# Decay attention in 64-token chunks from the fifth step on, ahead of two mixture layers on one core

## The chip, the cores and the metric

The kernel runs on one NeuronCore of one Trainium2 chip. The time is the device time of one execution in microseconds (us); lower is better. Before the change the median of 3 runs is 934.72 us (934.62 to 934.89).

## The reference: what is computed

There are 4 batches, 8 heads, 768 tokens, head size 48. Attention is a recurrence with a decaying state; its output, reordered to 3072 tokens of 384 numbers, goes through two feed-forward layers of width 2048.

```python
for t in range(S):                       # S = 768
    cur = einsum('bhd,bhe->bhde', u * kt, vt)
    y[:, :, t] = einsum('bhd,bhde->bhe', rt, state + cur)
    state = w * state + einsum('bhd,bhe->bhde', kt, vt)
x = y.transpose(0, 2, 1, 3).reshape(3072, 384)
h = x @ w_in;   x = relu(h)**2 @ w_out           # layer 1
h = x @ w_in2;  out = (h - tanh(h)) @ w_out2     # layer 2
```

The program doesn't walk token by token. It cuts the tokens into chunks. Within a chunk, token t sees token s < t through a masked score matrix (r times powers of w, against k times inverse powers), itself through r·(u*k) on the diagonal, and all earlier chunks through the state.

## The kernel before, in words

**Blocks and steps.** The 3072 tokens form 6 blocks j of 512 tokens; a block holds the same 128-token chunk of all 4 batches. Attention is done in 24 steps i, each one chunk of 128 tokens of one batch; step i belongs to block i // 4. A step has two halves d = 2i and 2i+1, each with two pairs of heads. In a pair one head lies on partitions 0 to 47 and the other on 64 to 111.

**Layers.** For each block and each of 16 slices f of the hidden width, `gemm1` (L496) makes h with 9 matmuls of 512 columns, ScalarE and another engine turn h into a high part `ghi` and a low part `glo`, and `gemm2_1` (L536) adds 9 matmuls into three accumulators. One such f of one block is a unit. The program goes through all units of layer 1 and then all of layer 2 (L646), and `gemm1` is issued one or two units ahead of its `gemm2`. In block 0 of layer 1 the weights are also unpacked on the way (`conv0` and `conv2` on ScalarE, L84 and L101; `conv1` on VectorE, L92 and L93; `conv3`, L107, on VectorE or GpSimd). `act1_low` (L525) makes `glo` on VectorE in the first and last block; in blocks 1 to 4 GpSimd makes it (L516).

**Attention in the units.** The first four steps run ahead of everything (`att_c0`, `att_e0`). Block j's units contain the steps of block j+1: in the units f = 0, 1, 3, 4, 6, 7, 9, 10 one half step d each. A half step issues:

- `att_a` (L253, L254): k and r times the tables of powers `tk` and `tr`, on VectorE. From d = 18 on, `att_split` (L272 to L279) also splits both into high and low fp32r parts, on ScalarE and VectorE.
- `att_b`: the scores. To d = 17 four fp32 matmuls of 128 columns (L300), the two heads of a pair on different rows of the array and into different PSUM banks; from d = 18 on six fp32r matmuls of 256 columns (L290).
- `att_s`, `att_d` (L308, L324): the diagonal, a reduction on VectorE and a product with the identity on GpSimd, written to `am`. `att_m` (L342, L335) copies the scores over `am` where the mask `low` is set, on VectorE.
- `att_c`: the output y. Two matmuls with the state `sbd`, a 112x112 matrix with the two heads' states on its diagonal (L422), four with `am` and v (L429), and, except in the last block, four that make the chunk's own k·v (L438).
- `att_e`: y goes to x in high and low parts (L455, L457), and the state is decayed and added to by four VectorE instructions of 48x48 (L463). `pack` moves the last pair of heads to its rows by DMA (L477).

`att_u`, `att_r`, `att_k` (L229, L232, L237) multiply the natural-order r and k by u, k and the decay table; they are put in a list by `nat_push` and taken off one per unit by `nat_pop`.

**What sets the order.** The order is written out by hand (`manual_schedule`); every engine takes its instructions in that order. PSUM banks are fixed: 0 to 2 the accumulators, 3 and 4 h, 5 to 7 attention.

The half step in a unit of block 0 reads:

```python
if att:
    att_c(d); att_e(d); loads(d); pack(d)
gemm2_1(j, f)
if att and d + 2 < NDALL:
    att_b(d + 2); att_dm(d + 2)
```

Of the kernel before, what the change touches and what calls it, by code (L numbers as in the profile page):

```python
# [25 lines left out]
def decay_attention_moe_moe_kernel(  # L26
# [90 lines left out]

    at_ctx = ExitStack()
# [3 lines left out]
    sbd = [ac.tile([GP, NP, GP], F32, name=f"sbd{o}") for o in range(TPB)]  # L122
    zero = ac.tile([GP, GP], BF16, name="zero")
    ident = ac.tile([128, 128], F32, name="ident")
    low = ac.tile([128, 128], F32, name="low")
    ub = ac.tile([128, DM], F32, name="ub")
    kt_tab = ac.tile([128, H, D], F32, name="kt_tab")
# [45 lines left out]

    def table_b():
# [4 lines left out]
        nc.scalar.activation(out=wdec, in_=vtab[:, :, C - 1:C], func=AF.Copy)  # L179
# [6 lines left out]
    def table_c():  # L186
# [12 lines left out]
        tv = kt_tab.rearrange("p (P two) d -> p two P d", two=2)  # L199
# [3 lines left out]
    def fill(n):  # L203
        t = bank(1, "warm")
        for _ in range(n):
            nc.tensor.matmul(t[0:GP, 0:256], lhsT=zero, rhs=low[0:GP].bitcast(BF16), start=True, stop=True)

    def setup_pool():
# [19 lines left out]
    def att_u(i, eng):  # L228
        eng.tensor_tensor(flat(rn_t[i]), flat(rn_t[i]), ub, op=ALU.mult)  # L229

    def att_r(i, eng):
        eng.tensor_tensor(flat(rn_t[i]), flat(rn_t[i]), flat(kv_t[i][:, 0]), op=ALU.mult)  # L232

    def att_k(i, eng):
        kn = flat(kv_t[i][:, 0])
        if i // TPB != NCH - 1:
            eng.tensor_tensor(kn, kn, flat(kt_tab), op=ALU.mult)  # L237

    nat_q = []

    def nat_push(i, eng):
        if i < NTAU:
            nat_q.extend([(att_u, i, eng), (att_r, i, eng), (att_k, i, nc.gpsimd)])

    def nat_pop(n=1):
        for _ in range(min(n, len(nat_q))):
            fn, i, eng = nat_q.pop(0)
            fn(i, eng)

    def att_a(d, eng=None):  # L250
        i, e = divmod(d, 2)
# [8 lines left out]
    def open_split():  # L260
        t = cv.tile([128, 2 * DM, 2], F32R, tag="raw", name="fr", bufs=3).rearrange("p x two -> p (x two)")
        nc.gpsimd.memset(t[0:GP, 512:1536].bitcast(F32), 0.0)
        ks = t[0:GP, 0:512].rearrange("p (x z s) -> p x z s", x=2, z=2)
        rs = t[0:GP, 512:1536].rearrange("p (x z a t) -> p x z a t", x=2, z=2, a=2)
        fr.append((ks, rs))

    def att_split(d):
        i, e = divmod(d, 2)
        q = slice(2 * e, 2 * e + 2)
        ks, rs = fr[d % 3]  # L270
        r, k = rk_t[i][:, 0, q], rk_t[i][:, 1, q]
        nc.scalar.activation(out=ks[:, 0], in_=k, func=AF.Copy)  # L272
        nc.vector.tensor_tensor(ks[:, 1], k, ks[:, 0].bitcast(F32), op=ALU.subtract)  # L273
        for a in range(2):
            s = slice(64 * a, 64 * a + D)
# [72 lines left out]
    def att_dm(d):  # L348
        if d % 2 == 0:
            att_s(d // 2)  # L350
# [602 lines left out]
```

## Time and profile before

| | us |
|---|---|
| median of 3 runs | 934.72 |
| profiled execution | 935.4 |
| its span, first to last instruction | 933.7 |
| TensorE busy | 907.2 (97%) |
| VectorE busy | 729.7 (78%) |
| ScalarE busy | 642.6 (69%) |
| GpSimd busy | 251.2 (27%) |
| mean granted TensorE clock | 0.989 of full speed |

The span falls into stretches: to about 41 us the first four attention steps run with little else, to 122 us block 0 of layer 1 runs with its weights being unpacked, to 473 us blocks 1 to 4 run with attention steps in them, to 527 us the last block of layer 1, and from there layer 2. Attention after the change is in the stretch from about 37 us to 473 us. PE is TensorE in the rows, DVE VectorE, ACT ScalarE, POOL GpSimd. An fp32 matmul shows as two records, so a group of 4 matmuls is x8; fp32r and bf16 matmuls show as one.

### The profile page before, as it was taken

To read this page: it belongs to the slowest core of one execution; us is meant where nothing else is said; L and a number is where in the kernel's file an instruction comes from. 1 tells how busy PE (TensorE), PEld (TensorE's weight loads), DVE (VectorE), ACT (ScalarE), POOL (GpSimd) and SP (SyncE) were. 2 spreads that over 40 slices of the span, in tenths; PEclk is the share of its full clock that TensorE was granted. 3 is DMA by queue.
4 is the path that set the end of the run, shared out by engine and by line. 5 is a ranking of instruction groups with operands and counts; after the bars stand their busy time and mean duration, and the time that the engine had idled before them with its cause. 6 is when DMAs were issued, how large, how long until landed. Compare 5 with 4: busy or idle time off the path is not lost.

```text
span 933.7 us, 13137 instructions
## 1 busy us (share of the span) xinstructions
PE 907.2 (97%) x4748; PEld 745.8 (80%) x4748; DVE 729.7 (78%) x1201; ACT 642.6 (69%) x1150; POOL 251.2 (27%) x216
## 2 busy tenths in 40 slices
PE   6889999999999999999999999999999999999998
PEld 6666778888888788888888778888888888888886
DVE  6898866882874678173167789999999999999997
ACT  3655665455554555554478797898888988988986
POOL 5832425552654445353202011001001001000000
PEclk7999999999999999999999999999999999999999
DMA  8845422221311212110446210010010100100000
GB/s 239 253 148 191 151 83 85 79 68 37 95 55 50 81 54 95 38 50 10 174 149 222 68 57 11 1 57 12 24 33 12 57 12 1 57 12 1 35 1 34
DMA packets 28801, 67.50 MB, mean 72 GB/s; under 512 B 4929, under 2 KB 11969, under 8 KB 28737
## 3 DMA queue, kind: packets, MB, share of 16 engines
q1 hardware_dynamic: 28592, 66.47, 21.9%
q8 instruction: 37, 0.61, 0.3%
q10 hardware_dynamic: 144, 0.20, 0.1%
q14 instruction: 28, 0.22, 0.1%
HBM read 55.25 MB, written 9.44 MB: 69 GB/s over the span
## 4 chain that ended last, share of the span: by engine, by line
PE 86%; DVE 7%; ACT 3%; DMA 1%; issue 1%; POOL 1%; SPq 0%; DVEq 0%; ACTq 0%; POOLq 0%
PE h L496 39%; PE acc L536 20%; PE o L646 20%; PE sc L290 2%; PE y L429 2%; PE y L422 2%; DMA kvt<-in_nat_dram 1%; DVE am L342 1%; DVE rkt L254 1%; PE sc L300 1%; DVE rkt L253 1%; DVE glo L525 1%; PE y L438 1%; DVE hy L592 1%; DVE raw L93 0%
## 5 line engine op out<-in xcount | busy, mean ns | idle before, releaser
L496 PE MATMUL h<-xt,w 128*128 128x512 f32 x864 | 215.6, 394 | 0.0
L496 PE MATMUL h<-xs,w 128*128 128x512 f32 x864 | 211.4, 389 | 0.0
L496 PEld LDWEIGHTS h<-xs,w 128*128 128x128 f32 x864 | 162.2, 188 | 34.0
L496 PEld LDWEIGHTS h<-xt,w 128*128 128x128 f32 x864 | 161.0, 190 | 33.5
L510 ACT ACTIVATE g<-h 128x512 f32<-128x512 f32 x96 | 57.2, 596 | 146.9 <-PE h L496 146.8
L536 PE MATMUL acc<-ghi,w 128*128 128x512 f32 x576 | 153.3, 398 | 0.3 <-ACT x2s L552 0.3
L646 PE MATMUL o<-ghi,w 128*128 128x512 f32 x576 | 148.8, 390 | 0.3 <-ACT ghi L617 0.3
L646 PEld LDWEIGHTS o<-ghi,w 128*128 128x128 f32 x576 | 107.7, 188 | 24.0 <-ACT ob L657 1.3
L536 PEld LDWEIGHTS acc<-ghi,w 128*128 128x128 f32 x576 | 104.9, 188 | 23.8 <-ACT g L510 1.1
L516 POOL TENSOR_TENSOR glo<-g,ghi 128x512 fp32r<-128x512 f32 x64 | 85.8, 1340 | 136.1 <-ACT ghi L513 61.8
L569 POOL TENSOR_TENSOR xs<-x2f,xs 128x512 fp32r<-128x512 f32 x18 | 24.4, 1354 | 316.6 <-DVE xs L568 316.6
L536 PE MATMUL acc<-glo,w 128*128 128x512 f32 x288 | 84.2, 394 | 6.8 <-DVE glo L525 6.8
L593 ACT ACTIVATE th<-h 128x512 f32<-128x512 f32 x96 | 57.5, 599 | 41.9 <-DVE hy L592 41.9
L646 PE MATMUL o<-glo,w 128*128 128x512 f32 x288 | 84.2, 394 | 2.0 <-DVE glo L623 1.9
L606 DVE SCALAR_TENSOR_TENSOR hy<-q,hy 128x512 f32<-128x512 f32 x96 | 78.2, 814 | 0.1
L592 DVE SCALAR_TENSOR_TENSOR hy<-h,y 128x512 f32<-128x512 f32 x96 | 66.0, 687 | 13.5 <-ACT y L590 13.4
L324 POOL TENSOR_TENSOR am<-ident,bt 128x512 f32<-128x512 f32 x44 | 50.0, 1137 | 90.4 <-DVE bt L308 69.6
L273 DVE TENSOR_TENSOR fr<-rkt,fr 112x256 fp32r<-112x256 f32 x30 | 38.8, 1294 | 42.7 <-ACT fr L272 42.7
L596 DVE TENSOR_TENSOR th<-h,th 128x512 f32<-128x512 f32 x96 | 66.2, 689 | 5.9 <-ACT th L593 0.7
L611 DVE COPY_PREDICATED hy<-mask,th 128x512 f32<-128x512 uint8 x96 | 70.8, 737 | 0.0
L536 PEld LDWEIGHTS acc<-glo,w 128*128 128x128 f32 x288 | 53.8, 188 | 20.7 <-DVE glo L525 9.8
L594 ACT ACTIVATE q<-y,ba 128x512 f32<-128x512 f32 x96 | 68.7, 715 | 0.0
(105 smaller groups left out, 1380.1 us busy)
## 6 DMA issues: line engine op xcount, KB each, us to landing
raw<-in_w_dram SPq DMA_DIRECT2D x32, 768.0 KB, 4.3
rkt<-in_rk_dram SPq DMA_DIRECT2D x23, 448.0 KB, 4.3
kvt<-in_nat_dram SPq DMA_DIRECT2D x23, 384.0 KB, 4.6
x2d<-x2s SPq DMA_DIRECT2D x18, 256.0 KB, 2.3
x2f<-x2d SPq DMA_DIRECT2D x18, 256.0 KB, 3.0
out_dram<-ob SPq DMA_DIRECT2D x18, 256.0 KB, 2.2
rnt<-in_nat_dram SPq DMA_DIRECT2D x23, 192.0 KB, 2.5
xt<-ys SPq DMA_DIRECT2D x120, 16.0 KB, 1.8
```

The costliest lines, as they stand in the source:

```text
L324: nc.gpsimd.tensor_tensor(am_t[d].rearrange("p (a z) t -> p a z t", a=2), ident[:, None, None, :].to_broadcast([128, 2, 2, C]), hd.to_broa ...
L496: nc.tensor.matmul(h, lhsT=w_in(layer, f, part, kk), rhs=x[:, xpart, kk, :], start=(n == 0), stop=(n == 3 * KK - 1),)
L510: nc.scalar.activation(out=g, in_=h, func=AF.Relu)
L516: nc.gpsimd.tensor_tensor(lo, g, hi.bitcast(F32), op=ALU.subtract)
L536: nc.tensor.matmul(acc[j][m], lhsT=w_out(1, f, part, m * 128, (m + 1) * 128), rhs=g, start=(f == 0 and n == 0), stop=(f == NF - 1 and n == 2),
L592: nc.vector.scalar_tensor_tensor(out=hy, in0=h, scalar=PK, in1=y, op0=ALU.mult, op1=ALU.mult)
L593: nc.scalar.activation(out=th, in_=h, func=AF.Tanh)
L594: nc.scalar.activation(out=q1, in_=y, func=AF.Square, bias=p2["ba"], scale=1.0)
L596: nc.vector.tensor_tensor(th, h, th, op=ALU.subtract)
L606: nc.vector.scalar_tensor_tensor(out=hy, in0=q2, scalar=PD, in1=hy, op0=ALU.add, op1=ALU.mult)
L611: nc.vector.copy_predicated(hy, mask, th)
L646: nc.tensor.matmul(acc[j][m], lhsT=w_out(2, f, part, m * 128, (m + 1) * 128), rhs=g, start=(f == 0 and n == 0), stop=(f == NF - 1 and n == 2),
```

## The change

From step 4 on a step is done in one go and not in two halves, and its 128 tokens are cut into two subchunks c of 64. Steps 0 to 3 keep the old code under the names `lead_*`. For the others:

- **Scores** (`att_b`): 16 fp32 matmuls (4 pairs, 2 subchunks, 2 heads) of 48 rows by 64 by 64 columns. The two heads of a pair are on different rows and different column halves of the array, and write the two halves of one PSUM bank (5).
- **k·v of each subchunk** (`att_v`): 16 fp32 matmuls of 64 rows by 64 by 48 columns into bank 6.
- **Output** (`att_c`): 16 fp32 matmuls of 64 by 64 columns. The state and v are stacked in one stationary tile `vs` (state on one head's 48 partitions, v of the 64 tokens on the other 64), and decayed r and the masked scores in one moving tile `ra`, so that one matmul gives both terms. Bank 7.
- **State** (`state_0`, `state_1`): kept as 112 x 4 x 48. VectorE decays and adds it in four instructions of 112x192, and ScalarE copies it into `vs` (four of 48x192).
- `att_a` is one VectorE product for k and two for r; the splitting into fp32r parts is gone. `att_d` writes the diagonal into `ra` (two GpSimd products of 64x512), `att_m` copies scores over it (two of 64x512).
- Visits are at f = 1, 4, 7, 10: `att_b` and `att_v` of step i+1, then `att_c` of step i, all in front of that unit's `gemm2`. `att_a` and `state_0` of step i+2 are issued two units after a visit, at f = 3, 6, 9 and 0. `nat_push` also lists `att_s` and `att_d`, and `nat_pop` takes two per unit.
- v and k come in separate transfers (5 a step in place of 3), and the first four steps' inputs lie in tiles that later hold weights, no longer in the rotating buffers. `table_d` makes a decay table for 64 tokens; VectorE clears the padding of the new tiles at the start.

The core of the diff:

```diff
-    sbd = [ac.tile([GP, NP, GP], F32, name=f"sbd{o}") for o in range(TPB)]
+    L = C // 2
+    GPS = NP * D
...
+    vs_p = [ac.tile([128, 2, VW], F32, name=f"vs{q}") for q in range(NV)]
+    kn_p = [ac.tile([128, VW], F32, name=f"kn{q}") for q in range(2)]
+    ra_p = [ac.tile([128, 2, NP, 2, L], F32, name=f"ra{q}") for q in range(2)]
...
+            nc.sync.dma_start(out=rk_t[i], in_=rk[i])
+            nc.sync.dma_start(out=rn_t[i], in_=nat[i, :, 0])
+            nc.sync.dma_start(out=kn_t[i][:, 0:DM], in_=nat[i, :, 1])
+            for a in range(2):
+                q = slice(64 * (1 - a), 64 * (2 - a))
+                nc.sync.dma_start(out=vs_t[i][q, a, 0:DM], in_=nat[i, q, 2])
...
+        k = sub(rk_t[i][:, 1])
+        win = slice(L // 2, C - L // 2)
+        (eng or nc.vector).tensor_tensor(k, k, tab(tk[:, :, win], GP), op=ALU.mult)
+        for a in range(2):
+            q = slice(64 * a, 64 * a + D)
+            nc.vector.tensor_tensor(ra_t[i][q, a], sub(rk_t[i][q, 0]), tab(tr[q][:, :, win], D), op=ALU.mult)
...
+            nat_q.extend([
+                lambda: att_u(i, G), lambda: att_r(i, G), lambda: att_s(i),
+                lambda: att_k(i, G), lambda: att_d(i, 0), lambda: att_d(i, 1),
+            ])
...
+    def att_b(i):
+        sc_t[i] = sc = pbank(i, 0, "sc").rearrange("p (P c t) -> p P c t", P=NP, c=2)
+        for p in range(NP):
+            for c in range(2):
+                for a in range(2):
+                    q = slice(64 * a, 64 * a + D)
+                    nc.tensor.matmul(
+                        sc[half(a), p, c, :], lhsT=rk_t[i][q, 1, p, c * L:(c + 1) * L], rhs=ra_t[i][q, a, p, c, :],
+                        start=True, stop=True,
+                    )
...
+    def att_v(i):
+        pv_t[i] = pv = pbank(i, 1, "pv")[:, 0:2 * GPS].rearrange("p (c P d) -> p c P d", c=2, P=NP)
+        for c in range(2):
+            for p in range(NP):
+                x = (c * NP + p) * D
+                for a in range(2):
+                    nc.tensor.matmul(
+                        pv[64 * a:64 * a + 64, c, p, :],
+                        lhsT=kn_t[i][half(a), x:x + 64], rhs=vs_t[i][half(a), a, x:x + D],
+                        start=True, stop=True,
+                    )
...
+    def state_1(i):
+        pv = pv_t.pop(i)[0:GP]
+        s = a2.tile([GP, NP, D], F32, tag="s1", name="s1", bufs=1)
+        nc.vector.tensor_tensor(s, dec_t.pop(i), pv[:, 0], op=ALU.add)
+        put_state(i, 1, s)
+        if i // TPB < NCH - 1:
+            m = st_m[i % TPB]
+            decay(m, s)
+            nc.vector.tensor_tensor(m, m, pv[:, 1], op=ALU.add)
...
+    def att_c(i):
+        y_t[i] = y = pbank(i, 2, "y").rearrange("p (P c t) -> p P c t", P=NP, c=2)
+        for p in range(NP):
+            for c in range(2):
+                for a in range(2):
+                    n = GP if a else 128
+                    x = (c * NP + p) * D
+                    nc.tensor.matmul(
+                        y[64 * a:64 * a + 64, p, c, :], lhsT=vs_t[i][0:n, a, x:x + 64], rhs=ra_t[i][0:n, a, p, c, :],
+                        start=True, stop=True,
+                    )
...
+            if layer == 1 and j + 1 < NB and f - 2 in (-2, 1, 4, 7):
+                i = TPB * (j + 1) + visit.get(f - 2, -1) + 2
+                if i < NTAU:
+                    att_a(i)
+                    state_0(i)
             if att:
-                if j == 0:
-                    a_to(min(d + 3, DR - 1))
-                att_c(d)
-                att_e(d)
-                loads(d)
-                pack(d)
+                i = TPB * (j + 1) + visit[f]
+                if i + 1 < NTAU:
+                    att_b(i + 1)
+                    att_v(i + 1)
+                att_c(i)
+                att_e(i)
+                pack(i)
+                load(i + 3)
...
-            if att and d + 2 < NDALL:
-                att_b(d + 2)
-                att_dm(d + 2)
-                if d % 2 == 0:
-                    nat_push(d // 2 + 2, G)
+            if att and i + 1 < NTAU:
+                att_m(i + 1)
+                state_1(i + 1)
+                nat_push(i + 2)
```

How TensorE's order changes: in block 1, before the change, a half step's scores stand between two units and its output behind the next `gemm1`:

```order
L536 MATMUL acc_2272<-glo,w_6_816 128x512
L290 MATMUL sc<-fr 128x256 x6
L496 MATMUL h<-xt,w_9_996 128x512 x9
L422 MATMUL y<-rkt,sbd_89 112x128 x2
L429 MATMUL y<-am,kvt 48x128 x4
L438 MATMUL y<-kvt 48x48 x4
L536 MATMUL acc_2270<-ghi,w_7_895 128x512
```

This comes eight times a block. At the same place after the change there is one piece, four times a block:

```order
L619 MATMUL acc_1558<-glo,w_6_858 128x512
L579 MATMUL h<-xt,w_9_1051 128x512 x9
L351 MATMUL sc<-ra_105,rkt 64x64 x16
L362 MATMUL pv<-vs_101,kn_103 64x48 x16
L413 MATMUL y<-ra_104,vs_100 64x64 x16
L619 MATMUL acc_1556<-ghi,w_7_971 128x512
```

The scores and the k·v of one step now stand directly ahead of the output of the step before it, and there are 48 small matmuls a step where there were 32 (12 of 256 columns and 20 of 48 or 128).

VectorE's order where block 0 begins, before the change (`bt` is the diagonal of the step, `glo` the low part that unit 0's `gemm2` reads):

```order
L308 TENSOR_REDUCE bt<-rnt 128x8
L253 TENSOR_TENSOR rkt<-rkt,tk 112x256
L254 TENSOR_TENSOR rkt<-rkt,tr 112x256
...
L93 SCALAR_TENSOR_TENSOR raw<-raw 128x768
L342 COPY_PREDICATED am<-low,sc 128x256 x4
L232 TENSOR_TENSOR rnt<-rnt,kvt 128x384
L525 TENSOR_TENSOR glo<-g,ghi 128x512
```

And after it:

```order
L293 TENSOR_REDUCE bt<-rnt 128x8
L319 TENSOR_TENSOR rkt<-rkt,tk 112x512
L322 TENSOR_TENSOR ra_104<-rkt,tr 48x512 x2
L385 TENSOR_TENSOR dec<-st,wdec 112x192
...
L372 COPY_PREDICATED ra_104<-low,sc 64x512 x2
L399 TENSOR_TENSOR s_596<-dec,pv 112x192
L385 TENSOR_TENSOR st<-s_596,wdec 112x192
L404 TENSOR_TENSOR st<-st,pv 112x192
L293 TENSOR_REDUCE bt<-rnt 128x8
L608 TENSOR_TENSOR glo<-g,ghi 128x512
```

The product L232 of step 5, which VectorE did itself, is now GpSimd's, and the reduction that reads it stands in front of unit 0's `glo`.

GpSimd's order at the same place, after the change (L107 is `conv3` of slice 2, then `att_u` and `att_r` of step 5):

```order
L303 TENSOR_TENSOR ra_104<-ident,bt 64x512 x2
L285 TENSOR_TENSOR kn_102<-kn_102,kt_tab 128x384
L107 TENSOR_TENSOR w_2_611<-raw,w_2_611 128x768
L277 TENSOR_TENSOR rnt<-rnt,ub 128x384
L282 TENSOR_TENSOR rnt<-rnt,kn_103 128x384
L285 TENSOR_TENSOR kn_103<-kn_103,kt_tab 128x384
```

Both products of step 5 now stand behind that `conv3`; before, L229 of step 5 was done in the lead stage and L232 by VectorE.

## Rows read from the trace of the kernel before

**Rows 1.** Stretches: length, busy PE, PEld, DVE, ACT, POOL; clock, DMA share, GB/s.
```profile
41.00:122.00 81.00, 72.70 (x451) 55.73 (x448) 73.24 (x134) 44.86 (x73) 30.76 (x25) 0.96 0.55 183
141.00:389.00 248.00, 247.65 (x1489) 207.63 (x1488) 159.67 (x291) 128.38 (x258) 127.75 (x107) 1.00 0.21 66
```

**Rows 2.** Timeline of PE, block 1, three units: start, length, what, count.
```profile
141.81 2.20 PE L496 MATMUL h<-xt,w 128*128 128x512 f32 x9
143.85 0.60 PE L422 MATMUL y<-rkt,sbd 112*112 112x128 f32 x4
144.38 0.64 PE L429 MATMUL y<-am,kvt 128*48 128x128 f32 x8
...
145.13 1.64 PE L536 MATMUL acc<-ghi,w 128*128 128x512 f32 x6
...
156.31 1.52 PE L536 MATMUL acc<-ghi,w 128*128 128x512 f32 x6
...
158.35 2.20 PE L496 MATMUL h<-xt,w 128*128 128x512 f32 x9
```

**Rows 3.** Timeline of PE in block 4, from one step to the next.
```profile
392.11 0.60 PE L422 MATMUL y<-rkt,sbd 112*112 112x128 f32 x4
...
408.36 0.60 PE L422 MATMUL y<-rkt,sbd 112*112 112x128 f32 x4
```

**Rows 4.** Timeline of PE in the first four steps, small matmuls at full clock.
```profile
24.91 0.45 PE L385 MATMUL y<-am,vz 128*64 128x128 f32 x4
...
26.27 0.58 PE L397 MATMUL pt<-kvt 128*48 128x48 f32 x16
26.79 0.43 PE L206 MATMUL warm<-low,zero 112*112 112x256 bf16 x2
```

**Rows 5.** Timeline of PE in block 0, three units with their two half steps.
```profile
101.32 1.52 PE L536 MATMUL acc<-ghi,w 128*128 128x512 f32 x6
103.55 0.96 PE L536 MATMUL acc<-glo,w 128*128 128x512 f32 x3 [0.71 <-DVE glo L525]
...
107.70 1.64 PE L536 MATMUL acc<-ghi,w 128*128 128x512 f32 x6
...
109.95 0.71 PE L300 MATMUL sc<-rkt 48*128 48x128 f32 x8
110.60 2.34 PE L496 MATMUL h<-xt,w 128*128 128x512 f32 x9
112.77 0.60 PE L422 MATMUL y<-rkt,sbd 112*112 112x128 f32 x4
...
119.13 1.52 PE L536 MATMUL acc<-ghi,w 128*128 128x512 f32 x6
```

**Rows 6.** DVE groups from 41 to 122 us: busy us, mean ns, idle before.
```profile
L342 DVE COPY_PREDICATED am<-low,sc 128x256 f32<-128x256 uint32 x20 | 7.7, 441 | 5.3 <-POOL am L324 5.3
L463 DVE SCALAR_TENSOR_TENSOR sbd<-sbd,wdec,y 48x48 f32<-48x48 f32 x32 | 7.0, 260 | 0.1
L253 DVE TENSOR_TENSOR rkt<-rkt,tk 112x256 f32<-112x256 f32 x9 | 6.2, 694 | 0.0
```

**Rows 7.** Timeline of DVE: its first instructions, and an `att_a` product over 512 elements.
```profile
6.78 1.85 DVE L166 TENSOR_TENSOR vtab<-vtab 112x4 f32<-112x4 f32 x7 [6.78 <-DMA vtab<-in_w_dram]
...
10.54 0.69 DVE L253 TENSOR_TENSOR rkt<-rkt,tk 112x512 f32<-112x512 f32 x1
```

**Rows 8.** Timeline of PE and POOL where block 0 begins.
```profile
48.90 0.97 PE L536 MATMUL acc<-glo,w 128*128 128x512 f32 x3 [0.76 <-DVE glo L525]
...
52.58 3.24 PE L496 MATMUL h<-xt,w 128*128 128x512 f32 x9
...
45.95 1.87 POOL L107 TENSOR_TENSOR w<-raw,w 128x768 fp32r<-128x768 f32 x1 [1.83 <-DVE am L342]
```

**Rows 9.** POOL groups from 41 to 122 us.
```profile
L232 POOL TENSOR_TENSOR rnt<-rnt,kvt 128x384 f32<-128x384 f32 x4 | 6.1, 1518 | 0.0
L229 POOL TENSOR_TENSOR rnt<-rnt,ub 128x384 f32<-128x384 f32 x4 | 4.0, 1006 | 0.0
```

More of the change, by code (lines that the diff above doesn't have):

```diff
@@ new lines, in att_m, with put_state @@
+    def att_m(i):
+        sc = sc_t.pop(i)
+        for a in range(2):
+            q = half(a)
+            nc.vector.copy_predicated(
+                ra_t[i][q, a].rearrange("p P c t -> p (P c) t"),
+                low[q, q].bitcast(U32)[:, None, :].to_broadcast([64, 2 * NP, L]),
+                sc[q].rearrange("p P c t -> p (P c) t"),
+            )
+    def put_state(i, c, src):
+        for a in range(2):
+            q = slice(64 * a, 64 * a + D)
+            dst = vs_t[i][q, a, c * GPS:(c + 1) * GPS].rearrange("p (P d) -> p P d", P=NP)
+            nc.scalar.activation(out=dst, in_=src[q], func=AF.Copy)
@@ L225, in flat, with pack @@
+    def pack(i):
+        j, o = divmod(i, TPB)
+        x, ys = xt[j], ys_t.pop(i)
+        ts = slice(o * C, (o + 1) * C)
+        for kk in range(KK):
+            for a in range(2):
+                nc.sync.dma_start(
+                    out=x[64 * a + D:64 * a + 64, :, kk, ts].bitcast(F32),
+                    in_=ys[64 * a + 16 * kk:64 * a + 16 * kk + 16, :, 0, :].bitcast(F32),
+                )
     def flat(ap):
         return ap.rearrange("p h d -> p (h d)")
-    def att_u(i, eng):
-        eng.tensor_tensor(flat(rn_t[i]), flat(rn_t[i]), ub, op=ALU.mult)
@@ L260, in open_split @@
[L260 to L275, printed above, removed]
-            nc.scalar.activation(out=rs[s, 0, :, a], in_=r[s], func=AF.Copy)
-        for a in range(2):
-            s = slice(64 * a, 64 * a + D)
-            nc.vector.tensor_tensor(rs[s, 1, :, a], r[s], rs[s, 0, :, a].bitcast(F32), op=ALU.subtract)
@@ L297, in att_b, with lead_a, lead_b @@
+    def lead_a(i, eng=None):
+        (eng or nc.vector).tensor_tensor(rk_t[i][:, 1], rk_t[i][:, 1], tk, op=ALU.mult)
+        nc.vector.tensor_tensor(rk_t[i][:, 0], rk_t[i][:, 0], tr, op=ALU.mult)
+    sc0 = {}
+    def lead_b(d):
+        i, e = divmod(d, 2)
+        b0 = 3 if d % 2 else 5
+        sc0[d] = sc = [bank(b0 + a, "sc") for a in range(2)]
         for z in range(2):
@@ L699, in decay_attention_moe_moe_kernel @@
         table_a()
-        load_rk(0)
-        load_rn(0)
-        nc.scalar.dma_start(out=ub, in_=u.to_broadcast([128, DM]))
-        load_kv(0)
-        load_rk(1)
-        load_rn(1)
-        load_kv(1)
-        load_rk(2)
-        load_rn(2)
-        load_kv(2)
-        load_w(1, 0)
-        first_block()
+        clear()
+        for i in range(TPB):
+            first(i)
+            if i == 2:
+                load_w(1, 0)
+        for a in range(2):
+            nc.scalar.dma_start(out=ub[half(a)], in_=u[1:2, a * GPS:(a + 1) * GPS].to_broadcast([64, GPS]))
         load_w(1, 1)
@@ L793, in decay_attention_moe_moe_kernel @@
         conv0(1, 2)
-        rs(4)
-        att_d(ND)
-        att_d(ND + 1)
+        att_s(4)
+        att_d(4, 0)
+        att_d(4, 1)
         front(0)
-        na[0] = ND
-        a_to(ND + 1)
-        att_b(ND)
+        att_a(4)
+        state_0(4)
         att_k(4, G)
+        att_b(4)
+        att_v(4)
         conv1(1, 2)
-        att_m(ND)
+        att_m(4)
+        state_1(4)
+        nat_push(5)
         load_w(1, 4)
-        load_rk(6)
-        load_kv(6)
-        load_rn(6)
+        load(6)
         conv2(1, 2)
```

454 lines of the change are left out of this document (210 added, 244 removed).

## The prediction

> **What bounds the kernel now.** I read the busy times by stretch first, since the attention that changes lies in only some of them, and then TensorE's timeline in each. Look at two rows [rows 1]. From 141 to 389 us (blocks 1 to 3, with attention) TensorE is busy 247.65 of 248 us and nothing else is near that: whatever time an attention step takes on TensorE is paid in full, and the others' work is free up to some slack. From 41 to 122 us (block 0) VectorE is busy 73.24 of 81 us and TensorE 72.70: the two hold each other up by turns, so saved TensorE time pays only as far as VectorE follows. From 527 us on no attention is left and nothing changes.
>
> What does one step cost on TensorE today? A unit without attention takes 2.04 us for `gemm1` (141.81 to 143.85) and 2.04 for `gemm2` (156.31 to 158.35), 4.08 together [rows 2]. Three units with the two half steps last from 141.81 to 158.35, 16.54; less 3 x 4.08 = 12.24 that leaves 4.30 a step, with all costs of going in and out of the small matmuls. In block 4, whose attention has no k·v, the period is 16.25 (392.11 to 408.36) [rows 3], so 4.01. In block 0 it is 17.81 (101.32 to 119.13) with 0.71 of waiting for `glo` [rows 5]: 17.81 - 0.71 - 12.24 = 4.86.
>
> **TensorE after the change.** A step has 48 fp32 matmuls: 16 scores of 64 columns, 16 k·v of 48, 16 outputs of 64. They come in 24 pairs, one matmul of each on the upper and one on the lower half of the array. The lead shows such pairs at full clock, on column halves: 24 records of 128 columns from 24.91 to 26.27, six pairs, 0.227 each; 16 records of 48 columns from 26.27 to 26.79, four pairs, 0.130 each [rows 4]. With 64 columns a pair costs 0.130 if the short ones are held by the number of instructions, or 0.130 + 16/80 x 0.097 = 0.149 on the line between the two; I take 0.140, in between, both ends being near. Sum: 16 x 0.140 + 8 x 0.130 = 3.28.
>
> Going in and out: ahead of the scores L300 a `gemm2` lasts 2.25 (107.70 to 109.95) and the `gemm1` behind them 2.17 (110.60 to 112.77) [rows 5], against 2.04 each: 0.34 for one burst on half arrays. The new step has one burst, with a change inside it, from tiles of half the rows to tiles of all rows; I take 0.42. A step is then 3.70.
>
> Twelve steps in blocks 1 to 3 save 0.60 each and four in block 4 save 0.31 each (they now make a k·v that they did without): 7.2 + 1.2 = 8.4 us.
>
> Bounds of this term. At best 24 x 0.130 + 0.34 = 3.46 a step: 12 x 0.84 + 4 x 0.55 = 12.3 saved. At worst the pairs of the scores and the k·v, which differ in rows as well as columns, don't overlap: an unpaired matmul of 128 columns takes 0.53 / 2 = 0.265 (L422, 143.85 to 144.38) [rows 2], half of that for 64 columns and 0.10 for 48. That is 16 x 0.133 + 16 x 0.10 + 8 x 0.140 + 0.42 = 5.27, a loss of 12 x 0.97 + 4 x 1.26 = 16.7. The trace does show row pairs, L300: 8 records in 0.65 us, 0.16 a matmul [rows 5], much below 0.265, so the good end is the nearer one.
>
> Here the Trainium skill speaks against the change. "TensorEngine Tiling (Array Packing)", section Tiling Modes, says that changing the tiling mode drains TensorE, and a new step changes it three times (into half tiles, to full-row tiles, out). This trace agrees that a change isn't free: the 0.34 above for in and out [rows 5]. If every change cost the whole 0.34, the step would be 3.28 + 1.02 = 4.30, and the first twelve would save nothing.
>
> **Block 0.** VectorE per step, from its groups [rows 6]: it loses the wait for GpSimd's diagonal, 5.3 us in five steps, 1.06 each, since `att_d` now stands a unit earlier. Eight small state instructions (7.0 us in four steps, 1.75) become four of 112x192, between 0.26 (0.69 x 192/512 [rows 7]) and 0.44 each; I take 1.2 together. The mask copies are the same number of elements. `att_a` was four products, 0.694 each by L253; it becomes three over 512 elements, between 0.69 [rows 7] and twice 0.694, so 2.1 to 4.2 against 2.8; I take 3.0. VectorE gains about 1.4 a step, between 0.1 less than nothing and 2.9. TensorE alone would need 12.24 + 3.70 = 15.94 for three units in place of 17.81, so no more than 1.9 can come of it. I take 1.0 for each of three periods: 3 us.
>
> Where block 0 begins a wait is added. The reduction of step 5 on VectorE must now wait for GpSimd's `att_u` and `att_r`, which stand behind `conv3` of slice 2. Behind that reduction are queued unit 0's `glo`, and behind it three matmuls, `gemm1` of unit 2 and the next scores. From rows: `conv3` ends at 45.95 + 1.87 = 47.82 [rows 8]; 1.0 and 1.5 for the two products [rows 9] give 50.3, reduction and `glo` some 0.5 and 0.7 by element count [rows 7], 51.5. Before, `glo` was read at 48.90 and `gemm1` of unit 2 began at 52.58, because the scores between waited too [rows 8]. After, the three matmuls end at about 52.2 and `gemm1` follows; but by then half an output (1.28, 143.85 to 145.13) and half the scores (0.65) are not yet done, and a k·v (1.04) is: 0.9 behind, 0.5 net. On ScalarE the copies of the new state wait for `state_1` and hold `conv2` of slice 2 behind them; 0.5 for that. Together 1 us lost.
>
> **At nothing.** ScalarE's four state copies a step: it is busy 128.38 of 248 us [rows 1] and loses the six splitting copies; without slack 1 us a step. GpSimd, 127.75 of 248, keeps its products. Five transfers a step for three: they run three steps ahead. The clearing of new tiles, twelve instructions on VectorE, lies in the 6.78 us in which it waits for w [rows 7]; at 0.69 each they would stick out by 1.5 us. `table_d`, some 0.5 us of matmuls, precedes warm-up matmuls that fill time; uncovered it costs that.
>
> **The sum.** 935.4 - 8.4 - 3 + 1 = 925.0 for the profiled execution (span 933.7 and 1.7 around it). That execution is 0.7 above the median of 934.72; so 924.3 for the median.
>
> **The rivals.**
> 1. *The two row tiles of a pair run one after the other* (slower). L300's two heads go into two banks; the new pairs write two halves of one bank, which no row of this trace shows. The place is every `att_b` and `att_v`, the price the worst end above: 16.7 in blocks 1 to 4 and 4 x (5.27 - 4.86) = 1.6 in block 0, with none of its gain: 935.4 + 18.3 - 0.7 = 953. It decides from a price of 0.17 for these 16 pairs, where the step costs 4.3 again (16 x 0.17 + 8 x 0.14 + 0.42). For it: those two banks. Against: the halves are disjoint partitions. The same page of the Trainium skill, section Restrictions and Gotchas, says that different row tiles cannot access one PSUM bank simultaneously; no run here shows it yet. Chance 0.12.
> 2. *Block 0 stalls at each visit* (slower). All of `att_a` is now done one unit before its scores, in VectorE's queue behind `conv1` and `conv3`; in a late queue TensorE waits, and its clock falls: after waits the `gemm1` at 52.58 took 3.24 for 2.20 [rows 2, 8]. Some 2 us of wait and 1.5 of half clock at four visits: 14. 935.4 - 8.4 + 14 = 941, less 0.7: 940. It decides from 2 us a visit. For it: VectorE is as busy there as TensorE. Against: it gets less work. Chance 0.11.
> 3. *Changes of shape eat the gain*: three changes at 0.34 each [rows 5], 3.28 + 1.02, steps of 4.30, no gain in blocks 1 to 3, 1.2 lost in block 4, a little won in block 0: 934 to 935. Chance 0.08.
> 4. *Better*: pairs at 0.130 and block 0 wholly relieved: 935.4 - 12.3 - 3 x 2.1 - 0.7 = 916. For it: in the lead the short pairs don't seem held by their columns. Chance 0.20.
>
> **How the numbers follow.** The forecast has 0.49, with 919 to 930 as its own range. A difference of 0.2% (1.9 us) is what can be told from none. Faster: forecast and rival 4, 0.69. Same: rival 3, 0.08. Slower: rivals 1 and 2, 0.23. The range 914 to 944 takes in all but rival 1 and some tails, 0.8.
>
> **What will show it.** In blocks 1 to 3 three units should last 15.9 us, not 16.54: scores and outputs 1.1 us each, k·v 1.04. Scores of 2 us mean rival 1; waits of the scores for `ra` in block 0, and a granted clock below 0.96 there, rival 2; lengthened `gemm1` and `gemm2` around the burst, rival 3. The prediction is wrong in its main term if the step isn't between 3.46 and 4.3.

## The result and the profile after

The changed kernel takes 944.09 us (median of 4 runs, 943.92 to 944.94) against 934.81 for the kernel before on the same chip (4 runs): ratio 1.0099, interval 1.0082 to 1.0117. It is slower by 9.3 us. The profiled execution has a span of 942.1 us and a mean granted clock of 0.976.

The same two stretches as in [rows 1], now of the changed kernel (length; busy PE, PEld, DVE, ACT, POOL; clock, DMA share, GB/s):

```profile
41.00:122.00 81.00, 62.97 (x520) 52.94 (x521) 62.50 (x82) 39.55 (x70) 29.57 (x22) 0.83 0.43 138
141.00:389.00 248.00, 245.17 (x2054) 203.19 (x2053) 95.50 (x157) 124.36 (x235) 124.24 (x107) 1.00 0.25 71
```

In the first, block 0, the clock is 0.83 for 0.96, and both engines that held each other up before are busy for less of the stretch: TensorE 62.97 us for 72.70, VectorE 62.50 for 73.24. That is no gain, for the stretch now holds less of block 0. Three turns of three units each, first before and then now, compare like with like (columns as above):

```profile
62.76:119.13 56.37, 52.89 (x332) 41.12 (x331) 50.17 (x94) 32.65 (x54) 18.42 (x15) 0.97 0.54 176
71.28:139.78 68.50, 55.14 (x452) 46.49 (x451) 56.09 (x73) 36.72 (x64) 21.61 (x15) 0.88 0.48 155
```

A turn took 18.79 us and takes 22.83; VectorE was busy for 16.72 of it and is for 18.70. In the second stretch, from 141 to 389 us, which now begins with the last 19 us of block 0, TensorE is busy 245.17 us at the full clock. So the trace is best cut where block 0 ends. The `gemm1` that began at 141.81 before [rows 2] begins at 160.58 now: 18.8 us late. From there to the last instruction it was 791.9 us (933.7 - 141.8) and is 781.5 (942.1 - 160.6): 10.4 won. The difference, 8.4, is that of the two spans.

**Where it wins.** TensorE's timeline in block 1, three units and one step, as in [rows 2]:

```profile
165.87 2.20 PE L579 MATMUL h<-xt,w 128*128 128x512 f32 x9
168.00 1.15 PE L351 MATMUL sc<-ra,rkt 48*64 48x64 f32 x32
168.98 1.09 PE L362 MATMUL pv<-vs,kn 64*64 64x48 f32 x32
170.00 1.15 PE L413 MATMUL y<-ra,vs 128*64 128x64 f32 x32
171.08 1.66 PE L619 MATMUL acc<-ghi,w 128*128 128x512 f32 x6
...
173.27 2.21 PE L579 MATMUL h<-xt,w 128*128 128x512 f32 x9
...
181.44 2.20 PE L579 MATMUL h<-xt,w 128*128 128x512 f32 x9
```

165.87 to 181.44 is 15.57; less 12.24 for three units, a step costs 3.33, not 4.30. The three stages start 0.98, 1.02 and 1.08 apart: 0.122, 0.128 and 0.135 for each of eight pairs.

**Where it loses.** TensorE's timeline at one visit of block 0:

```profile
84.02 0.45 PE L351 MATMUL sc<-ra,rkt 48*64 48x64 f32 x2 [4.42 <-issue]
84.69 1.86 PE L351 MATMUL sc<-ra,rkt 48*64 48x64 f32 x29 [0.23 <-DVE ra L322]
...
86.39 1.95 PE L362 MATMUL pv<-vs,kn 64*64 64x48 f32 x31
88.27 1.97 PE L413 MATMUL y<-ra,vs 128*64 128x64 f32 x32
90.17 1.92 PE L619 MATMUL acc<-ghi,w 128*128 128x512 f32 x6
```

The scores wait 4.42 us, for which the profile names no releaser ("issue"); early_a below, which only moves `att_a`, takes such waits away. Then they run at the lower of the clock's two levels (granted 0.50 from 84.02 to 90.17, so 1.2 GHz; 1.00, or 2.4 GHz, in the burst of block 1): 1.86, 1.95 and 1.97 for what takes 1.15, 1.09 and 1.15 there, so some 2.4 us more. The four visits of block 0 wait 2.91, 4.42, 4.17 and 3.79. VectorE over the same turn, from one mask copy (L372) to the next:

```profile
68.68 1.48 DVE L372 COPY_PREDICATED ra<-low,sc 64x512 f32<-64x512 uint32 x2
...
76.31 1.79 DVE L107 TENSOR_TENSOR w<-raw,w 128x768 fp32r<-128x768 f32 x1
78.03 1.41 DVE L92 TENSOR_SCALAR raw<-raw 128x768 uint32<-128x768 uint32 x1
79.48 1.63 DVE L93 SCALAR_TENSOR_TENSOR raw<-raw 128x768 uint32<-128x768 uint32 x1
81.03 1.49 DVE L319 TENSOR_TENSOR rkt<-rkt,tk 112x512 f32<-112x512 f32 x1
82.44 2.20 DVE L322 TENSOR_TENSOR ra<-rkt,tr 48x512 f32<-48x512 f32 x2
...
91.00 0.29 DVE L432 TENSOR_TENSOR ys<-y,ys 112x128 fp32r<-112x128 f32 x1 [3.04 <-ACT xt L430]
...
91.79 1.48 DVE L372 COPY_PREDICATED ra<-low,sc 64x512 f32<-64x512 uint32 x2
...
96.01 0.96 DVE L107 TENSOR_TENSOR w<-raw,w 128x768 fp32r<-128x768 f32 x1 [1.12 <-ACT w L101]
```

And GpSimd beside it (its products of [rows 9], now behind the two `att_d`; before, the same five stood mixed):

```profile
75.94 3.08 POOL L303 TENSOR_TENSOR ra<-ident,bt 64x512 f32<-64x512 f32 x2 [14.87 <-DVE bt L293]
...
82.05 1.33 POOL L285 TENSOR_TENSOR kn<-kn,kt_tab 128x384 f32<-128x384 f32 x1
```

This turn takes 23.11 us (68.68 to 91.79). The 17.81 of [rows 5] is the better of two kinds that the kernel before had; the turn ahead of it took 20.75 (80.57 to 101.32), with a wait for `glo` in it:

```profile
80.57 1.52 PE L536 MATMUL acc<-ghi,w 128*128 128x512 f32 x6
84.14 1.37 PE L536 MATMUL acc<-glo,w 128*128 128x512 f32 x3 [2.05 <-DVE glo L525]
```

The turn now is a ring: `att_m` and the state on VectorE, the conversions, `att_a`, then scores, k·v and output on TensorE, then ScalarE's copies of y, for which VectorE idles 3.04 us, and `att_m` again. `att_a` is done by 84.67, 15.99 after the masks began; the other 7.12 pass until the next masks.

**The start.** VectorE's reduction of step 5 waited 4.88 us for GpSimd, so `glo` of unit 0 was begun at 53.21 and `gemm1` of unit 2 began at 55.20, against 52.58 in [rows 8]. VectorE, then TensorE:

```profile
52.74 0.55 DVE L293 TENSOR_REDUCE bt<-rnt 128x8 f32<-128x384 f32 x1 [4.88 <-POOL rnt L282]
53.21 1.13 DVE L608 TENSOR_TENSOR glo<-g,ghi 128x512 fp32r<-128x512 f32 x1
```

```profile
54.40 0.96 PE L619 MATMUL acc<-glo,w 128*128 128x512 f32 x3 [2.74 <-DVE glo L608]
55.20 2.21 PE L579 MATMUL h<-xt,w 128*128 128x512 f32 x9
```

So of the 18.8 us 2.6 are lost where block 0 begins, 5.9 more up to the first of the three turns (55.20 to 71.28, before 52.58 to 62.76) and 12.1 in these turns (68.50 less 56.37); behind them 1.9 come back.

### The profile page after: what moved, and what is told of

It is laid out like the page before. It is cut to its first block, busy times and chain, and to the rows that moved or that the text cites. A ratio compares the mean times of both kernels' runs of the same rounds, so it can differ in the third digit from the quotient of the medians.

```text
span 942.1 us, 14863 instructions
## 1 busy us (share of the span) xinstructions
PE 898.2 (95%) x5688; PEld 739.4 (78%) x5688; DVE 650.8 (69%) x1016; ACT 632.9 (67%) x1121; POOL 251.1 (27%) x214
## 4 chain that ended last, share of the span: by engine, by line
PE 80%; DVE 10%; ACT 4%; DMA 2%; POOL 2%; issue 1%; ACTq 0%; DVEq 0%; POOLq 0%
PE h L579 36%; PE o L729 19%; PE acc L619 17%; PE y L413 3%; PE sc L351 2%; PE pv L362 2%; DVE raw L93 1%; DVE ra L322 1%; DVE w L107 1%; DVE raw L92 1%; DMA x2d<-x2s 1%; DMA first_kv<-in_nat_dram 1%; DVE rkt L319 1%; DMA vtab<-in_w_dram 1%; DVE ra L372 1%
## 5 line engine op out<-in xcount | busy, mean ns | idle before, releaser
L579 PE MATMUL h<-xt,w 128*128 128x512 f32 x864 | 213.2, 392 | 0.0
L579 PEld LDWEIGHTS h<-xt,w 128*128 128x128 f32 x864 | 163.2, 189 | 34.4
L619 PEld LDWEIGHTS acc<-ghi,w 128*128 128x128 f32 x576 | 106.9, 189 | 28.0 <-ACT x2s L635 5.2
L432 DVE TENSOR_TENSOR ys<-y,ys 112x128 fp32r<-112x128 f32 x20 | 5.8, 292 | 149.9 <-ACT xt L430 149.9
L680 ACT ACTIVATE q<-y,bb 128x512 f32<-128x512 f32 x96 | 68.5, 713 | 0.0
L683 ACT ACTIVATE mask<-y,bm 128x512 uint8<-128x512 f32 x96 | 68.3, 711 | 0.0
```

Of the source, the lines that this page charges most:

```text
L579: nc.tensor.matmul(h, lhsT=w_in(layer, f, part, kk), rhs=x[:, xpart, kk, :], start=(n == 0), stop=(n == 3 * KK - 1),)
L619: nc.tensor.matmul(acc[j][m], lhsT=w_out(1, f, part, m * 128, (m + 1) * 128), rhs=g, start=(f == 0 and n == 0), stop=(f == NF - 1 and n == 2),
L680: nc.scalar.activation(out=q2, in_=y, func=AF.Square, bias=p2["bb"], scale=1.0)
L683: nc.scalar.activation(out=mask, in_=y, func=AF.Sign, bias=p2["bm"], scale=1.0)
```

## The experiments

Three theories of block 0, so named in the expectations: **R**, the ring of waits sets the turn, and any link cut shortens it; **W**, VectorE has too much to do there, its instructions stretched while GpSimd works beside them; **C**, the low clock of the small matmuls is the loss. The kernel before measured 934.7 to 935.3 beside all runs, and the ratios are to it. All edits but those named otherwise are in block 0 alone.

| kernel | us | ratio, interval |
|---|---|---|
| after_again | 944.13 | 1.0096, 1.0081 to 1.0111 |
| c_first | 934.22 | 0.9984, 0.9969 to 1.0000 |
| b_late | 935.02 | 0.9996, 0.9983 to 1.0009 |
| early_a | 934.68 | 0.9995, 0.9985 to 1.0004 |
| warm | 936.47 | 1.0015, 1.0006 to 1.0024 |
| diag | 934.02 | 0.9989, 0.9980 to 0.9997 |
| noprod | 933.08 | 0.9986, 0.9973 to 1.0000 |
| diag_noprod | 928.80 | 0.9932, 0.9916 to 0.9948 |
| late_early | 931.56 | 0.9960, 0.9945 to 0.9975 |
| early_noprod | 928.44 | 0.9926, 0.9911 to 0.9941 |
| early_start | 932.32 | 0.9971, 0.9960 to 0.9982 |
| early_diag | 929.95 | 0.9946, 0.9927 to 0.9964 |
| early_start_diag | 929.59 | 0.9940, 0.9928 to 0.9952 |
| late_early_start_vec | 930.86 | 0.9949, 0.9936 to 0.9962 |
| late_early_start_diag | 927.07 | 0.9917, 0.9904 to 0.9930 |
| best_noprod | 927.09 | 0.9910, 0.9893 to 0.9927 |

### Cutting the ring: c_first, b_late, early_a, warm

Output ahead of the next step's scores; scores and k·v behind `gemm2`; `att_a` one unit earlier; 40 fill matmuls ahead of the scores, to hold the clock.

```diff
# c_first (all diffs here are shortened)
+if j == 0: att_c(i)
 att_b(i + 1); att_v(i + 1)
-att_c(i)
+if j: att_c(i)
# b_late (late is j == 0)
-if i + 1 < NTAU:
+if i + 1 < NTAU and not late:
     att_b(i + 1); att_v(i + 1)
 att_c(i); att_e(i); pack(i)
...
 gemm2_1(j, f)
...
+if att and late:
+    att_b(i + 1); att_v(i + 1); load(i + 3)
# early_a (lag is 1 in block 0 but at f = 0, else 2)
-if layer == 1 and j + 1 < NB and f - 2 in (-2, 1, 4, 7):
+if layer == 1 and j + 1 < NB and f - lag(j, f) in (-2, 1, 4, 7):
# warm
+if j == 0: fill(40, 7)
 att_b(i + 1); att_v(i + 1)
```

> In block 0 only, att_c of step i is issued ahead of att_b and att_v of step i+1. Theory R (ring): in block 0 the scores wait for att_a at the end of VectorE's queue, the output waits behind the scores on TensorE, and VectorE's att_e waits for the output (3.0 us idle a visit), so the engines go round in a ring of 23.1 us for three units. With the output first, VectorE's idle time and the time of scores and k.v at half clock leave the ring: 3 to 5 us less at each of four visits, 926 to 933. Theory W (work): VectorE simply has too much to do in block 0, slowed by GpSimd's burst of products; order changes little: 942 to 944. Theory C (clock): the loss is the half clock after the waits; the waits stay, so does the half clock: 940 to 944.

> In block 0 only, att_b and att_v of step i+1 are issued behind that unit's gemm2, as the scores were before the change; att_c stays ahead of it. Theory R: the output no longer waits for att_a and the scores have 3 to 4 us more: the ring is open, 3 units at 17 to 18 us, 924 to 929. Theory W: 941 to 944. [...]

> In block 0 only, att_a and state_0 are issued one unit earlier (f = 2, 5, 8 in place of 3, 6, 9). Theory R: the scores find their operands, the 4.4 us waits at the scores go, but the glo and conv1 behind att_a come later by its 3.5 us, so a part comes back as waits for glo: 930 to 936. Theory W: the waits only move to glo: 942 to 944. Theory C: 936 to 942, since some waits get short.

> In block 0 forty warm-up matmuls of 256 columns (about 4.3 us) into the bank of y stand ahead of the scores of each visit, and leave no result; they fill TensorE's wait. Theory R: scores, k.v and output run at full clock (3.1 for 5.5 us) but the wait for att_a stays, 2 to 2.4 us less at each of four visits: 934 to 937. Theory C: the clock is all, the waits shrink with it: 928 to 932. Theory W: VectorE is the bound, so TensorE's clock gives nothing: 942 to 945.

Each takes 8 to 10 us off 944.1, at four different links, so the ring is shown; but the first two stop short of what R expected. In b_late TensorE waits for `glo` in place of `ra` (2.61, 2.75, 1.35 and 3.58 us at the four visits), since `glo` stands behind `att_a` in VectorE's queue, and behind the three longer waits its matmuls run slow there too. In early_a, where the visits after the first no longer wait for `ra`, a turn still takes 19.87 us, and VectorE is idle for 1.1 us of it, with GpSimd's work at its side. In warm the matmuls keep the clock, which tells what the clock is worth in a turn:

```profile
78.68 4.54 PE L256 MATMUL warm<-low,zero 112*128 112x256 bf16 x40
...
83.94 1.08 PE L351 MATMUL sc<-ra,rkt 48*64 48x64 f32 x29 [0.40 <-DVE ra L322]
...
84.90 1.10 PE L362 MATMUL pv<-vs,kn 64*64 64x48 f32 x31
85.93 1.15 PE L413 MATMUL y<-ra,vs 128*64 128x64 f32 x32
```

The scores still wait for `ra`, most of the time behind the fill, but the three stages take 1.1 each (granted clock 1.00), and the time falls by 7.6. So C is a part of the loss, not its beginning: the clock falls behind TensorE's waits.

### The neighbour: diag, noprod, diag_noprod

The order stays the changed kernel's; what GpSimd does beside VectorE is taken away, part by part.

```diff
# diag: att_d of steps 5 to 8
-nc.gpsimd.tensor_tensor(ra_t[i][q, a], ident[q, q][...], bt_t[i][q][...], op=ALU.mult)
+for p in range(NP):
+    for c in range(2):
+        nc.scalar.activation(out=ra_t[i][q, a, p, c], in_=ident[q, q], func=AF.Copy, scale=bt_t[i][q, c, p:p + 1])
# noprod: nat_push of steps 6 to 8 (a branch of its own in the program)
-lambda: att_u(i, G), lambda: att_r(i, G), lambda: att_s(i),
-lambda: att_k(i, G), lambda: att_d(i, 0), lambda: att_d(i, 1),
+lambda: None, lambda: None, lambda: att_s(i),
+lambda: None, lambda: att_d(i, 0), lambda: att_d(i, 1),
```

> The changed kernel in its own order, with only the two att_d of steps 5 to 8 on ScalarE (16 activations of 64x64 a step) in place of GpSimd. It asks what GpSimd's part of the change costs by itself. The contention theory: att_a and the conversions beside the second att_d take their lengths alone (0.68 and 1.38 for att_a's 1.49 and 2.20), 1.5 to 2 us off each of three turns of the ring: 937 to 940. Rival (the 4 us of activations stand in the ring's ScalarE part and eat that): 942 to 945.

> The changed kernel in its own order with only the products u, r, k of steps 6 to 8 left out (their terms are then not the reference's); att_d stays on GpSimd. With both neighbours gone the time was 928.8, with att_d alone gone 934.0. Contention theory: att_a behind the two att_d runs at its own lengths, 0.68 and 1.38, three of the five stretched instructions are stretched no more: 930 to 934. If att_d is the part that matters and the products matter only without it: 938 to 943.

> The changed kernel's own order with GpSimd silent in block 0's three periods: the two att_d of steps 5 to 8 on ScalarE, and the products u, r, k of steps 6 to 8 left out (their terms are then not the reference's). Moving att_d alone gave 10.1 us of the 18.8 that block 0 lost, and att_a still took 1.48 and 2.19 beside the products. Contention theory: att_a takes 0.68 and 1.38, a third conversion 0.96 for 1.66, 2.3 us off each of three periods: 926 to 929. Rival (what is left is the ring itself, the lengths of its links alone): 932 to 934.

Both parts alone give about what a cut gives (10.1 and 11.0 off 944.1), more for diag than either theory had expected, and both together 15.3: not the sum, since other links come next. VectorE of diag_noprod over the stretch shown above:

```profile
64.23 1.49 DVE L385 COPY_PREDICATED ra<-low,sc 64x512 f32<-64x512 uint32 x2
...
71.89 0.96 DVE L107 TENSOR_TENSOR w<-raw,w 128x768 fp32r<-128x768 f32 x1
72.77 0.56 DVE L92 TENSOR_SCALAR raw<-raw 128x768 uint32<-128x768 uint32 x1
73.36 0.96 DVE L93 SCALAR_TENSOR_TENSOR raw<-raw 128x768 uint32<-128x768 uint32 x1
74.23 0.68 DVE L326 TENSOR_TENSOR rkt<-rkt,tk 112x512 f32<-112x512 f32 x1
74.83 1.40 DVE L329 TENSOR_TENSOR ra<-rkt,tr 48x512 f32<-48x512 f32 x2
...
79.84 0.96 DVE L107 TENSOR_TENSOR w<-raw,w 128x768 fp32r<-128x768 f32 x1 [2.62 <-ACT w L101]
...
82.99 1.48 DVE L385 COPY_PREDICATED ra<-low,sc 64x512 f32<-64x512 uint32 x2
```

The same five lines take 4.56 for 8.52. From the masks to the end of `att_a` it is now 12.03 us (64.23 to 76.26) for 15.99: 3.96 less, which is the stretch alone. The first two turns are 18.76 and 18.74 for 23.11, and their scores wait under 1.1 us and run at full clock (the third is 21.26, with a wait of 2.22; GpSimd is at work again there, for step 9, and `att_a` takes 1.51 and 2.88). What holds a turn now is new: VectorE waits 2.62 for ScalarE's conversion, which stands behind the 16 activations. In noprod `att_d` still works beside L107 and L92, and only these two are stretched:

```profile
73.02 1.80 DVE L107 TENSOR_TENSOR w<-raw,w 128x768 fp32r<-128x768 f32 x1
74.74 1.42 DVE L92 TENSOR_SCALAR raw<-raw 128x768 uint32<-128x768 uint32 x1
76.19 0.96 DVE L93 SCALAR_TENSOR_TENSOR raw<-raw 128x768 uint32<-128x768 uint32 x1
```

The Trainium skill, "SBUF — State Buffer", section Who interferes with whom, says that a VectorE instruction with two SBUF inputs contends with a GpSimd instruction that reads SBUF. These rows agree: L107 takes 1.79 beside GpSimd and 0.96 without it. L92, with one input, which that sentence does not cover, is stretched as well, 1.41 for 0.56.

### The changed kernel once more: after_again

> The changed kernel itself once more, beside the others. Four edits at different places of its block 0 each took it from 944.1 to 934 to 935, so what they are compared with is measured again on their terms. If they act as told, it is 943.5 to 945 here too, with a period of 23 us in block 0. If 944 came from something else than its code, it is 933 to 936 with a period near 20.5.

944.13: the edits' gains are gains over the changed kernel as it is.

### Cuts and neighbour together

late_early is b_late and early_a at once; early_noprod and early_diag are early_a with the edits above. early_start adds the former start:

```diff
-nat_push(5)
-nat_pop(3); front(1); nat_pop(3)
+att_u(5, G)                         # in the lead, behind att_r(4, G)
+att_r(5, V); att_s(5); front(1)
+att_k(5, G); att_d(5, 0); att_d(5, 1)
```

> Both orders of block 0 at once: att_a and state_0 one unit earlier, and att_b and att_v of the next step behind gemm2. Each alone gave 934.7 and 935.0, against 944.1 for the changed kernel. Theory W (with the ring cut, VectorE's work in block 0, slowed while GpSimd works beside it, sets the period of three units at about 20 us): both together are worth no more than one, 933 to 936, and VectorE has no idle stretch of 1 us or more within a period. Theory R (order alone: each cut takes away a part of the wait, the rest goes with the other cut): 924 to 929, the period near 17.8 as in the kernel before.

> att_a one unit earlier, and GpSimd's three products (u, r, k) of steps 6 to 8 left out; their diagonal and state terms are then not the reference's. Theory W: VectorE loses the neighbour that lengthens its operations (L107 1.79 beside GpSimd against 0.95 alone in the changed kernel), about 2 to 2.5 us for each of three visits: 926 to 929. Theory R: GpSimd is off the chain, and the time stays that of the earlier att_a alone, 933 to 935.5.

> att_a one unit earlier, and the start of block 0 as before: att_u of step 5 on GpSimd behind att_r of step 4, att_r of step 5 on VectorE, att_s, then att_k and the two att_d behind the first front. In the changed kernel VectorE's reduction of step 5 waited 4.88 us for GpSimd, and glo of unit 0 with it. If that wait is on the path: 2 to 4 us less than the earlier att_a alone, 930.5 to 932.7. If block 0 is set by VectorE's work whatever its start (W in its strict form): the moved product adds 0.6 to VectorE and the time stays 934 to 936.

> att_a one unit earlier, and the diagonal att_d of steps 5 to 8 written by ScalarE (16 activations of 64x64 a step) in place of GpSimd's two products. Theory W: GpSimd's burst beside VectorE shrinks from about 8.3 to 4.6 us a step, VectorE's operations lose about half of what they are stretched by, 1 to 1.5 us a visit: 930 to 932. Rival (ScalarE, in the ring with its evacuations, puts_state and the first conv halves, pays about 3 us a step for the activations): 936 to 944. R without either: 934 to 935.5.

late_early's time falls between its two numbers, but its trace tells the theories apart. These are its first two mask copies in block 0:

```profile
65.85 1.50 DVE L372 COPY_PREDICATED ra<-low,sc 64x512 f32<-64x512 uint32 x2
...
85.72 1.49 DVE L372 COPY_PREDICATED ra<-low,sc 64x512 f32<-64x512 uint32 x2
```

Its turn is 19.87 us, no shorter than early_a's, and VectorE is idle for 1.1 us of it: with the ring cut, VectorE's stretched work sets the turn, as W says. The second cut's 3.1 us, which put the time below W's range, come ahead of the first masks (65.85, in early_a 68.72); for that first visit early_a leaves `att_a` at its old place.

The neighbour is worth 6.2 and 4.7 over early_a. Both numbers lie at or in W's ranges, but not for W's reason: 3.8 and 4.1 of them come ahead of the first masks too (64.94 and 64.65), and the turns only fall from 19.87 to 19.25 in early_noprod and to 18.98 and 19.56 in early_diag, not by the 1 to 2.5 us expected. VectorE is then busy for 16.3 us of early_noprod's turn, but waits 1.6 for y, and TensorE 1.8 for `glo`: another chain has taken over. The start's wait is on the path, 2.4 us.

In late_early_start_vec `att_d` of steps 5 to 8 is on VectorE (`nc.vector` in place of `nc.gpsimd`); the other two add up the diffs above.

> The earlier att_a, the former start of block 0, and ScalarE's diagonal, all three. Alone over the earlier att_a (934.7) the start gave 2.4 and the diagonal 4.7 us. If they sit at different places (the start ahead of the first visit, the contention in each period): 926.5 to 928.5. If the first period is bound by VectorE anyway and swallows the start's gain: 929 to 931.

> The earlier att_a, the later att_b and att_v, the former start, and the two att_d of steps 5 to 8 on VectorE itself. VectorE gets 1.4 us more a step by the length of its 64x512 operations alone (0.75 each), and loses its neighbour for 4.4 of the 8.6 us that GpSimd works beside it. Contention theory: 2 us less stretch against 1.4 more work, 0 to -1 us a visit over 929 (the later order and the start together): 926 to 929. If VectorE's own work alone is the bound and GpSimd costs it nothing: 932 to 934.

> All four: earlier att_a, later att_b and att_v, former start, ScalarE's diagonal. If the parts of block 0's loss (ring, start, contention) are what was named, block 0 is back near the 17.8 us of the kernel before for three units and blocks 1 to 4 keep their 10 us: 923 to 926. If with the contention halved the later order has nothing left to hide: as the other three together, 926.5 to 929.

> The fastest kernel so far (all four edits, 927.1) with the same products of steps 6 to 8 left out: what block 0 takes when neither the ring nor GpSimd is in its way. If contention is what is left of the loss: another 1.5 to 2 us in each of three periods, 921 to 923. If something else bounds a period there (VectorE's own work, TensorE's 16.8 us): 925 to 927.

With the diagonal gone from GpSimd the start's gain is swallowed (929.59 against 929.95). Putting it on VectorE lands between both numbers, 930.86. Its turns are 20.27 and 20.90, longer than late_early's, so in a turn the work added outweighs the stretch saved; both cuts and the start with GpSimd's diagonal, which would price the edit alone, were not run. All four edits give 927.07, faster than both kernels: 0.9917 of the time before. That is the second of its two expectations: the turns are 18.97 and 19.45, not 17.8, and so near the 18.79 that was the mean before. best_noprod shows what is left there: without the products too it is no faster, 927.09. There VectorE waits for ScalarE; VectorE, then ScalarE:

```profile
79.51 0.96 DVE L107 TENSOR_TENSOR w<-raw,w 128x768 fp32r<-128x768 f32 x1 [2.89 <-ACT w L101]
```

```profile
73.88 4.03 ACT L306 ACTIVATE ra<-ident,bt 64x64 f32<-64x64 f32 x16
```

So the 4.03 us of activations, the price of the edit, seem to have taken the stretch's place; no run without them tests it.

## Why the prediction was wrong, step by step

- **The steady step** was right, and mis-sized on the careful side: 3.33 for 3.70, and less than the 3.46 taken for the best. A pair costs 0.122 to 0.135 where 0.140 and 0.130 were taken, and 48 columns are no cheaper than 64. Going in and out costs 0.24 for 0.42: the `gemm1` ahead lasts 2.13 (165.87 to 168.00) and the `gemm2` behind 2.19, against 2.04 each. Block 4 saves 0.68 a step for 0.31. Twelve steps of 0.97 and four of 0.68 make 14.4. The term was 8.4 and came out at 10.4, for a wait at four block ends costs 3.5 (0.3 before; the page has it), and 0.6 more goes behind block 4, its cause open:

```profile
L619 PE MATMUL acc<-ghi,w 128*128 128x512 f32 x576 | 152.9, 396 | 3.5 <-ACT x2s L635 3.5
```

- **Rival 1**, row tiles of a pair serialized in one bank, did not happen: 0.122 a pair is less than one 64-column matmul alone by the prediction's estimate (0.133, half of an unpaired one of 128 columns), let alone two. The rule of one bank that the prediction sets beside this rival does not show here: the measurement decides. **Rival 3**, costly changes of shape, neither: going in and out costs the 0.24, and the change inside the burst has little room, since k·v and output together are 0.14 longer than two stages of 0.98. The rule that a change of the tiling mode drains TensorE (the Trainium skill, "TensorEngine Tiling (Array Packing)", section Tiling Modes) seems worth no more than these 0.4 us here.
- **Block 0 is the step that failed**: "VectorE gains about 1.4 a step", hence 3 us won; it lost 16. VectorE gained nothing: it is busy 2.0 us more in a turn (18.70 for 16.72). The wait for the diagonal did go, and the four state instructions take 1.40 for 1.80 (1.2 taken). But `att_a` was taken from a group mean, and a mean hides beside what an instruction runs. VectorE before, in block 0:

```profile
99.34 1.24 DVE L253 TENSOR_TENSOR rkt<-rkt,tk 112x256 f32<-112x256 f32 x1
...
109.16 0.42 DVE L253 TENSOR_TENSOR rkt<-rkt,tk 112x256 f32<-112x256 f32 x1
...
114.26 1.79 DVE L107 TENSOR_TENSOR w<-raw,w 128x768 fp32r<-128x768 f32 x1
115.98 1.35 DVE L92 TENSOR_SCALAR raw<-raw 128x768 uint32<-128x768 uint32 x1
117.37 1.65 DVE L93 SCALAR_TENSOR_TENSOR raw<-raw 128x768 uint32<-128x768 uint32 x1
```

The 0.694 of [rows 6] mixes 0.42 alone with 1.24 beside GpSimd. Alone, the four products took some 1.7, and the three new ones take 2.06 (0.68 and 1.38): not less. Now all of `att_a` stood in the window of GpSimd's burst and took 3.69 (3.0 taken); with the conversions ahead of it the stretch is 3.96 a turn. The last three lines show that the kernel before was stretched too, by 2.3 in that turn, so some 1.7 of the 3.96 are new. The rest of the loss goes with the ring, which the forecast's sum left out: late `att_a`, waiting scores, half clock, late y, idle VectorE. Its base was too good as well: 17.81 is one kind of turn, and the mean of three was 18.79.
- **Rival 2** named the place and the mechanism, `att_a` late in VectorE's queue and the clock falling, and gave it 0.11. Its price was near: 2 us of wait for 2.9 to 4.4, and 1.5 of clock for 2.4. What spoke against it, that VectorE gets less work, was not so, and in a ring it would not have decided.
- **The start** cost 2.6 for 1. `glo` was done at 54.34 (53.21 and 1.13), not 51.5. GpSimd's two products took 1.02 and 0.99, for 1.0 and 1.5, but `conv3` ahead of them began at 48.79, not 45.95, for it waited for ScalarE's `conv2`, behind the state copies. That hold-up was counted at 0.5 and is 2.8:

```profile
48.79 1.88 POOL L107 TENSOR_TENSOR w<-raw,w 128x768 fp32r<-128x768 f32 x1 [4.35 <-ACT w L101]
```

- **At nothing**: ScalarE's copies of the state hold up the conversion behind them (VectorE waits 1.12 there in a turn, before 0.38), inside the ring.

How the 18.8 us divide between stretch, ring and clock can't be told exactly: the parts overlap, and taking one away uncovers the next. Not tried was a diagonal made on none of VectorE, ScalarE and GpSimd.

## What to carry to other kernels

Where two engines hold each other up by turns, follow one turn of the ring in the timeline and add up its links; the sum of each engine's work says little. Take more than one turn as the base: here they were 17.81 and 20.75 long. Read the length of an instruction from where it will stand, with what runs beside it: the same VectorE product took 0.68 and 1.49 us. A stage that waits may also run on at a lower clock, so price a wait on TensorE with the slow matmuls behind it.

## What was not expected of the hardware

- Pairs of fp32 matmuls on disjoint quarters of the array, writing two halves of one PSUM bank, ran at 0.122 us a pair, with 64 and with 48 columns about alike.
- VectorE's products, conversions and a one-input `tensor_scalar` took 1.6 to 2.5 times as long beside GpSimd's products (1.79 for 0.96, 1.41 for 0.56, 1.49 for 0.68).
- Edits at unlike places of one ring each gave back 8 to 11 us; two together gave 12.5 (late_early) and 15.3 (diag_noprod), not the sum.
